# Batch 0's keys and queries loaded in full precision, 4096-byte output rows, and eight SBUF slots for expert weights that are copied or skipped

## The chip, the cores and the metric

The kernel runs on one core of a Trainium2 chip. The metric is device time in microseconds of one execution. The kernel before was run three times: 172.74, 174.44 and 174.59 us, median 174.44 us. One more execution was profiled.

## What is computed

There are two stages. The first is an attention in which 576 positions of each head are first averaged into 32 memory slots:

```python
a = softmax over positions of phi            # (8, 8, 576, 32)
k_m = einsum('bhsm,bhsd->bhmd', a, k)        # 32 averaged keys per head
v_m = einsum('bhsm,bhsd->bhmd', a, v)
attn = softmax(q @ k_m^T / 8)                # 576 x 32 per head
x = (attn @ v_m), heads side by side         # 4608 rows of 512
```

The second is a mixture of experts on the 4608 rows, with a dense branch beside it:

```python
y_dense = relu(x @ w1_dense) @ w2_dense
expert = argmax(x @ w_gate); gate = softmax(x @ w_gate)[expert]
y = y_dense + gate * (relu(x @ w1[expert]) @ w2[expert])
```

There are 8 batches, 8 heads of width 64, and 8 experts with weights 512 x 512. All inputs are float32.

## The kernel before

The work is cut by batch. Every batch goes through the same steps, and each step is a small function that is registered under a name. A long string, ORDER, lists the steps by hand: a token such as hd2:5 is hidden tile 2 of batch 5, and /A or /V picks ScalarE or VectorE for a copy. The program is issued in exactly this order, so the order of tokens is the order within each engine's queue; between engines semaphores decide.

The steps of one batch are these.

- Loads. Lphi (line 164) brings phi over SP's queue in float32. Lq, Lk and Lv (lines 188 and 181) bring q, k, v over the queue of GpSimd (called POOL in the profile), whose DMAs turn float32 into float16 as they go. Each row of such a load has 1152 bytes (phi) or 2304 bytes (q, k, v) at the source.
- e0, e1: ScalarE takes the exponential of phi (line 300). z, kv: TensorE sums it and its products with k and v (lines 311, 333), kvm divides. T, kTc, vTc turn the averaged keys and values (lines 355, 365).
- q0, q1, qT0, qT1: TensorE transposes q, a copy brings it to SBUF (line 114). s0, s1 are the scores (line 412), ET, Z, ln, inv and A their softmax (lines 425, 436, 449, 458, 463). A holds the attention weights; it stands for x, since the weights of the second stage are multiplied with v_m first.
- vg, pc, choose: the logits are vT times the gate weights. choose (lines 501 to 507) sums the logits over all memory slots of the batch and takes the expert with the largest sum. A register is loaded from its result (line 513), and steps w1 and w2 (lines 211, 218) load that expert's two matrices, 512 KB each after the cast, over POOL's queue with a dynamic address. Each matrix has two buffers.
- fd, vd and fe, ve fold v_m with the dense or the expert's first matrix (line 596). hd, Hd and he, He are the hidden layers (lines 609, 650, 652, 663), four tiles of 128 each; He multiplies the gate in. yd and ye are the second matrices (line 683): both halves accumulate into the same PSUM tile p_y of a chunk of 128 rows (the last one has 64). Y copies it to SBUF (lines 707, 709), o stores it over SP's queue (lines 718, 723).
- L, mxeq, ex, gates, pg, gB give the expert of every row, its gate, and whether it is the batch's expert. pn and flags count the rows that chose another one; if there are any, others(b) runs after the main part and adds the other experts' share. On the given inputs it does not run.

The tile pool of PSUM has two double banks ("big": p_q, p_kv, p_s, p_z, p_h, p_g), three single ones ("one": p_vw, p_y) and one small. VectorE, ScalarE and POOL work strictly in the order of their queues: an instruction that waits holds all behind it.

A values_load reads a register of one engine from SBUF. The load of w1 waits for it, and so does every load that stands behind it in POOL's queue.

Of the kernel before, what the change touches and what calls it, by code (L numbers as in the profile page):

```python
# [31 lines left out]
q1:3 He1:1 Lk:3 yd4:1 ye4:1 Lv:3 q0:3 Lphi:3 choose:2 A0:2 ye0:1 A1:2 ye1:1 L:2 Y4:1/A qT1:3/A
Y0:1/A ex:2 Y1:1/V mxeq:2 qT0:3/V hd1:2 yd3:1 yd2:1 e0:3 hd3:2 w1:2 ye3:1 e1:3 z:3 Hd1:2/A Hd3:2/A
gates:2 kv:3 pg:2 ye2:1 rz:3 gB:2/A kvm:3 Y3:1/A T:3 hd0:2 kTc:3/V w2:2 s1:3 Hd0:2/A fe:2 Y2:1/V
vTc:3/V Lq:4 ve1:2/V ET1:3 ve0:2/A hd2:2 s0:3 fd:3 Hd2:2/V vg:3 ET0:3 he2:2 He2:2 Z0:3 vd0:3/A yd0:2
ln0:3 vd1:3/V he0:2 he3:2 He0:2 yd1:2 He3:2 vgc:3 he1:2 Z1:3 pc:3 Lphi:5 Lphi:4 yd4:2 Lphi:6 He1:2
e0:5 ye4:2 inv0:3 e0:4 ye0:2 choose:3 ln1:3 q0:4 q1:4 inv1:3 A0:3 Y4:2/A e1:4 A1:3 Lk:4 qT1:4/V
qT0:4/V yd2:2 Y0:2/A L:3 ex:3 yd3:2 hd2:3 ye3:2 hd0:3 mxeq:3 ye2:2 gates:3 Hd2:3/V pg:3 Hd0:3/V z:4
e1:5 Y3:2/A gB:3/V rz:4 Y2:2/A Lv:4 w1:3 kv:4 kvm:4 hd1:3 hd3:3 T:4 e1:6 Hd1:3/A fe:3 ve1:3/V
kTc:4/V Hd3:3/A ye1:2 ve0:3/A Y1:2/A he3:3 he1:3 vTc:4/V He3:3 vg:4 fd:4 Lk:5 w2:3 He1:3 s1:4 yd4:3  # L40
ET1:4 vgc:4 vd1:4/A s0:4 ET0:4 vd0:4/V Lq:5 pc:4 he0:3 He0:3 yd3:3 Z0:4 ln0:4 inv0:4 he2:3 yd2:3
Lv:5 He2:3 A0:4 choose:4 Z1:4 ye2:3 ye3:3 ln1:4 q1:5 inv1:4 Lq:6 q0:5 A1:4 L:4 Y3:3/A qT1:5/V ex:4
mxeq:4 yd0:3 ye4:3 gates:4 qT0:5/A Y4:3/A kv:5 z:5 pg:4 e0:6 rz:5 yd1:3 kvm:5 gB:4/A T:5 kTc:5/A
Y2:3/V hd0:4 s1:5 ye1:3 ET1:5 vTc:5/V Hd0:4/V Z1:5 vg:5 s0:5 ln1:5 Y1:3/V w1:4 fe:4 hd3:4 ET0:5
# [22 lines left out]
def kernel(  # L67
# [795 lines left out]
```

## Time and profile before

| | |
|---|---|
| runs | 172.74 to 174.59 us, median 174.44 |
| profiled execution | 171.97 us, of which the span from first to last instruction is 170.3 |
| TensorE clock granted | 0.996 |
| TensorE busy | 143.5 us (84%), 2401 matmuls |
| VectorE, ScalarE, POOL busy | 101.0, 88.3, 32.2 us |
| POOL's DMA queue q0 | 22176 packets, 23.60 MB, 83.6% of 16 engines' span |
| SP's DMA queue q1 | 10056 packets, 14.11 MB, 24.0% |
| HBM read and written | 51.92 and 9.44 MB |

Bytes of a queue are counted where they are written, so a casting load counts half of what it reads. DMA shares are sums over packets in flight and can pass 1. PE in the profile is TensorE, PEld its weight load, DVE VectorE, ACT ScalarE.

### The profile page before, as it was taken

How to read it: one execution, taken by the hardware profiler on the slowest of the kernel's cores; microseconds unless marked ns; L12 is line 12 of the kernel's file. 1: busy time of each engine (PE TensorE's matmuls, PEld its weight loads, DVE VectorE, ACT ScalarE, POOL GpSimd, SP SyncE). 2: the span in 40 equal slices, each digit the busy share in tenths (PEclk: the TensorE clock that was granted, in tenths of full speed). 3: DMA queues.
4: the chain of work that ended last, by engine and by line, in shares of the span. 5: the costliest groups of instructions: out<-in, count | busy, mean ns of one | idle time of the engine just before them, and what ended most of it. 6: DMA issues, size and time to landing. Idle time of an engine off the chain costs nothing.

```text
span 170.3 us, 5557 instructions
## 1 busy us (share of the span) xinstructions
PE 143.5 (84%) x2401; PEld 84.8 (50%) x2401; DVE 101.0 (59%) x268; ACT 88.3 (52%) x153; POOL 32.2 (19%) x49
## 2 busy tenths in 40 slices
PE   4013779898999998999999989999699999999960
PEld 3012446465545655556655735565365655456430
DVE  0055275474795863688577856877477756476410
ACT  3130296887236665773666755443574674853130
POOL 7700009002600080008200600080030001200000
PEclk9999999999999999999999999999999999999998
DMA  4999999999999999999999999999999996899461
GB/s 121 300 235 209 206 207 195 205 204 208 199 207 219 246 332 228 243 207 174 203 206 209 187 201 212 289 365 237 208 208 207 259 386 251 111 229 396 190 224 45
DMA packets 32342, 38.18 MB, mean 224 GB/s; under 512 B 1588, under 2 KB 28212, under 8 KB 32312
## 3 DMA queue, kind: packets, MB, share of 16 engines
q0 software_dynamic: 22176, 23.60, 83.6%
q1 hardware_dynamic: 10056, 14.11, 24.0%
q8 instruction: 20, 0.33, 0.7%
q10 hardware_dynamic: 80, 0.07, 0.1%
q14 instruction: 10, 0.08, 0.1%
HBM read 51.92 MB, written 9.44 MB: 360 GB/s over the span
## 4 chain that ended last, share of the span: by engine, by line
PE 54%; DMA 30%; DVE 4%; issue 3%; POOL 2%; ACT 1%; POOLq 1%
PE p_y L683 26%; DMA w1e<-in_moe_w_dram 15%; PE p_h L609 14%; DMA kv<-in_k_dram 8%; DMA w2e<-in_moe_w_dram 7%; PE p_vw L596 3%; PE p_z L436 2%; PE p_s L412 2%; PE p_kv L333 2%; DVE HTe L663 1%; POOL q L188 1%; PE p_g L576 1%; DVE A L463 1%; PE p_q L390 1%; POOLq L513 1%
## 5 line engine op out<-in xcount | busy, mean ns | idle before, releaser
L683 PE MATMUL p_y<-w2d,HTd 128*128 128x512 f16 (+1 forms) x192 | 37.3, 346 | 0.0
L683 PE MATMUL p_y<-w2e,HTe 128*128 128x512 f16 (+1 forms) x192 | 36.7, 345 | 0.6 <-DMA w2e<-in_moe_w_dram 0.6
L663 DVE SCALAR_TENSOR_TENSOR HTe<-p_h,gB 128x576 f16<-128x576 f32 x32 | 23.5, 755 | 12.5 <-PE p_h L609 11.9
L211 POOL DMA_DIRECT2D w1e<-in_moe_w_dram x8 | 6.0, 746 | 112.1 <-DVE A L463 56.0
L609 PE MATMUL p_h<-A,vwd 128*128 128x288 f16 x128 | 22.1, 299 | 0.9 <-DVE qT L114 0.9
L707 ACT ACTIVATE y<-p_y 128x512 f32<-128x512 f32 (+1 forms) x25 | 13.8, 554 | 15.8 <-PE p_y L683 15.2
L683 PEld LDWEIGHTS <-HTe 128*128 128x128 f16 (+1 forms) x192 | 14.6, 101 | 13.7 <-issue 2.5
L683 PEld LDWEIGHTS <-HTd 128*128 128x128 f16 (+1 forms) x192 | 15.1, 101 | 11.6 <-issue 1.3
L609 PE MATMUL p_h<-A,vwe 128*128 128x288 f16 x128 | 19.5, 286 | 0.2 <-DVE HTd L652 0.2
L650 ACT ACTIVATE HTd<-p_h 128x576 f16<-128x576 f32 x21 | 13.4, 649 | 10.2 <-PE p_h L609 8.2
L300 ACT ACTIVATE E<-phi 128x576 f16<-128x576 f32 x16 | 10.5, 679 | 10.2 <-DMA phi<-in_phi_dram 9.5
L609 PEld LDWEIGHTS <-vwe 128*128 128x128 f16 x128 | 11.9, 97 | 5.8 <-issue 1.1
L609 PEld LDWEIGHTS <-vwd 128*128 128x128 f16 x128 | 11.3, 100 | 6.9 <-issue 2.4
L449 ACT ACTIVATE lnz<-p_z 128x576 f32<-128x576 f32 x16 | 10.3, 649 | 8.4 <-PE p_z L436 7.3
L709 DVE TENSOR_SCALAR y<-p_y 128x512 f32<-128x512 f32 (+1 forms) x15 | 9.5, 635 | 7.6 <-PE p_y L683 7.1
L425 ACT ACTIVATE ET<-p_s 128x576 f16<-128x576 f32 x16 | 10.2, 650 | 6.4 <-PE p_s L412 6.4
L114 DVE CAST vwe<-p_vw 128x512 f16<-128x512 f32 x12 | 8.0, 688 | 8.3 <-PE p_vw L596 8.3
L463 DVE TENSOR_TENSOR A<-ET,lnz 128x576 f16<-128x576 f16 x16 | 11.5, 744 | 0.3
L458 ACT ACTIVATE lnz<-lnz 128x576 f32<-128x576 f32 x16 | 10.7, 685 | 0.2
L114 ACT COPY qT<-p_q 128x1152 f16<-128x1152 f16 x7 | 7.7, 1114 | 4.1 <-PE p_q L390 4.1
L333 PE MATMUL p_kv<-kv,E 64*32 64x128 f16 x576 | 6.8, 232 | 3.1 <-DMA kv<-in_k_dram 3.1
L652 DVE TENSOR_SCALAR HTd<-p_h 128x576 f16<-128x576 f32 x11 | 8.3, 755 | 1.9 <-PE p_h L609 1.7
(86 smaller groups left out, 174.6 us busy)
## 6 DMA issues: line engine op xcount, KB each, us to landing
out_dram<-y SPq DMA_DIRECT2D x32, 256.0 KB, 4.8
q<-in_q_dram POOLq DMA_DIRECT2D x8, 576.0 KB, 12.1
kv<-in_v_dram POOLq DMA_DIRECT2D x8, 576.0 KB, 16.2
kv<-in_k_dram POOLq DMA_DIRECT2D x8, 576.0 KB, 14.3
w1e<-in_moe_w_dram POOLq DMA_DIRECT2D x8, 512.0 KB, 7.1
w2e<-in_moe_w_dram POOLq DMA_DIRECT2D x8, 512.0 KB, 11.6
phi<-in_phi_dram SPq DMA_DIRECT2D x7, 576.0 KB, 9.6
out_dram<-y SPq DMA_DIRECT2D x15, 64.0 KB, 4.2
```

What stands on the lines that cost most here:

```text
L114: (nc.scalar.copy if e == "A" else nc.vector.tensor_copy)(out=out, in_=in_)
L300: nc.scalar.activation(out=x["E"][:, :, hs].rearrange("p t j m -> p j t m"), in_=x["phi"][:, hs], func=AF.Exp,)
L333: nc.tensor.matmul(x["kvz"][M * j : M * j + M, a, 0 : 2 * Dh], lhsT=x["E"][rs, t, j], rhs=x["kv"][rs, :, j, t], start=(t == 0), stop=(t == ...
L425: nc.scalar.activation(out=st[b]["ET"][:, a].rearrange("m (p t) -> m p t", t=T), in_=st[b].pop(("ps", a)).rearrange("m (t p) -> m p t", t= ...
L449: nc.scalar.activation(out=st[b]["lnz"][:, a].rearrange("p (h c) -> p h c", h=2), in_=st[b].pop(("pz", a))[:, :, 0:HC], func=AF.Ln,)
L458: nc.scalar.activation(out=lnz, in_=lnz, func=AF.Exp, scale=-1.0)
L463: eng.tensor_mul(out=A[b][:, a], in0=st[b]["ET"][:, a], in1=st[b]["lnz"][:, a])
L609: nc.tensor.matmul(p_h[:, h, 0:HC], lhsT=vw[:, g, 128 * ft : 128 * ft + 128], rhs=a[:, g, HC * h : HC * h + HC], start=(g == 0), stop=(g = ...
L650: nc.scalar.activation(out=o, in_=p_h, func=AF.Relu)
L663: nc.vector.scalar_tensor_tensor(out=x["HTe"][:, ft].rearrange("p (h c) -> p h c", h=2), in0=x.pop(("pe", ft))[:, :, 0:HC], scalar=0.0, in ...
L683: nc.tensor.matmul(p_y[n * u : n * u + n, 0:w], lhsT=HT[:, ft, lo : lo + n], rhs=w2[:, ft, w * u : w * u + w], start=(half == 0 and ft == ...
L707: nc.scalar.activation(out=o, in_=p_y, func=AF.Copy, scale=1.0 / SC)
```

## The change

It has four parts, and the whole ORDER string is new.

1. Batch 0's q and k are no longer loaded by casting DMAs. Steps Fq0, Fq1, Fk0, Fk1 load them in halves in float32 over SP's queue, into buffers of the output tile; Cq0 casts on VectorE, Cq1, Ck0 and Ck1 cast on POOL. For batch 0 the sums over k and v are separate steps (kk, kmk, Tk and vv, kmv, Tv). Seven groups of 8 warm-up matmuls in place of two stand behind z:0. The gate weights are turned by ScalarE.
2. A stored row is 4096 bytes: a partition holds two neighbouring rows of the output. For that, chunk c of 128 rows takes every second of 256 columns of HT and A, and the gates of the chunk are written to PSUM at a stride of two.
3. W1 and W2 hold a slot for each of the 8 batches. choose also looks for the first earlier batch with the same expert; if there is one, both loads of the batch are skipped by a condition on their DMA. Steps rl, cw1 and cw2 then copy, for each batch from 1 on and on VectorE, from the slot found (its own, if nothing was found) to the batch's slot.
4. s0 and s1 become one step, s, with the matmuls of both interleaved. phi has two buffers in place of three, A has two in place of eight, and phi of batches 2, 3, 5, 6, 7 is loaded over POOL's queue. others(b) computes the attention again, as A is not kept.

The start of the new order:

```
Lv:0 Lphi1:0 cblk:0 Fq0:0 Lw1d:0 Lq:1 Lk:1 Lv:1 cid:0 Lwg:0 ciota:0 cones:0 Cq0:0/V Lphi0:0 e1:0
wgt:0/A wgm:0 e0:0 Fk0:0 Ck0:0/P Fk1:0 Ck1:0/P z:0 warm:0/8 warm:0/8 warm:0/8 warm:0/8 warm:0/8
warm:0/8 warm:0/8 rz:0 q0:0 Fq1:0 kk:0 kmk:0 Tk:0 vv:0 qT0:0/A ciotac:0 kTc:0/V wgc:0 kmv:0 Cq1:0/P
q1:0 Tv:0 qT1:0/V vTc:0/A vg:0 s:0 ET1:0 ET0:0 vgc:0 pc:0 Z1:0 fd:0 Z0:0 choose:0 ln1:0 inv1:0 ln0:0
inv0:0 vd0:0/V q0:1 q1:1 A1:0 vd1:0/A A0:0 qT0:1/V qT1:1/V Lphi:1/S hd2:0 e0:1 w1:0 e1:1 Lw2d:0 L:0
hd0:0 Hd2:0/A ex:0 Hd0:0/V mxeq:0 hd3:0 hd1:0 z:1 rz:1 gates:0 Hd3:0/A kv:1 kvm:1 T:1 w2:0 Hd1:0/A
vTc:1/V fd:1 kTc:1/A vd0:1/V s:1 vg:1 vgc:1 Lq:2 ET0:1 ET1:1 fe:0 pc:1 pg:0 vd1:1/A Z0:1 yd1:0
ve1:0/V ve0:0/V gB:0/A ln0:1 he3:0 he0:0 yd0:0 choose:1 He3:0 He0:0 he1:0 Lphi:2/P he2:0 yd3:0 He1:0
He2:0 w1:1 Z1:1 ln1:1 inv1:1 rl:1 inv0:1 A1:1 ye1:0 q0:2 ye3:0 ye0:0 A0:1 Y3:0/A e1:2 L:1 qT0:2/V
Y0:0/V cw1:1 Y1:0/V hd0:1 q1:2 yd4:0 e0:2 ye4:0 qT1:2/A ex:1 Y4:0/A yd2:0 mxeq:1 Hd0:1/A gates:1
...
```

POOL's queue after that holds, in order: w1:1, k:2, v:2, w2:1, phi:3, q:3, k:3, v:3, w1:2, w2:2, q:4, v:4, k:4, phi:5, w1:3, k:5, v:5, q:5, w2:3, w1:4, w2:4, q:6, v:6, phi:6, k:6, q:7, w1:5, w2:5, phi:7, v:7, k:7, w1:6, w2:6, w1:7, w2:7. The copies of w2:3 stand between kv:5 and q1:5 of TensorE's order, and the last tokens are again the store of the short chunk of batch 7.

The core of the diff:

```diff
-    A = [keep.tile([128, 2, S], F16, name=f"A{b}") for b in range(B)]
+    W1 = keep.tile([128, B, DT, F], F16)
+    W2 = keep.tile([128, B, FT, D], F16)
...
+    cols = [slice(256 * (c // 2) + c % 2, 256 * (c // 2) + 256, 2) for c in range(2 * NP)]
+    cols.append(slice(S - 128, S))
...
+    @step("Fk0", "Fk1", "Fq0", "Fq1")
+    def _(b, i, e):
+        if ("f", i[1]) not in st[b]:
+            st[b]["f", i[1]] = wk.tile([128, NJ, T * Dh], F32, tag="y", name="f" + i[1], bufs=NKEEP)
...
+        nc.sync.dma_start(out=st[b]["f", i[1]][:, hs], in_=rows(src[b])[:, hs])
...
+    def load_w1(out, e, cond=None):
         nc.gpsimd.dma_start(
+            out=out, in_=moe_w1[ds(e, 1)].rearrange("o (dt p) f -> p (o dt) f", p=128), cond=cond
...
+        if b and REUSE:
+            same = sm.tile([1, B], F32, tag="same", name="same")
+            nc.vector.scalar_tensor_tensor(
+                out=same[:, 0 : b + 1],
+                in0=em[0:1, 0 : b + 1],
+                scalar=emb[0:1],
+                in1=first[0:1, 0 : b + 1],
+                op0=ALU.is_equal,
+                op1=ALU.mult,
+            )
+            nc.vector.tensor_reduce(out=sel[0:1, 0:1], in_=same[:, 0 : b + 1], axis=AXX, op=ALU.min)
+            nc.vector.tensor_scalar(
+                out=e_i[b][:, 1:2], in0=sel[0:1, 0:1], scalar1=float(B), scalar2=None, op0=ALU.add
+            )
...
+        ev = nc.values_load(e_i[b][:, 0:1], engines=pool, min_val=0, max_val=E - 1)
+        cond = None
+        if b and REUSE:
+            cond = nc.values_load(e_i[b][:, 1:2], engines=pool, min_val=0, max_val=b) >= b
+        st[b]["ev"] = ev, cond
+        load_w1(W1[:, b], ev, cond)
...
+    @step("rl")
+    def _(b, i, e):
+        st[b]["slot"] = nc.values_load(
+            e_i[b][:, 1:2], engines=(ENG.DVE,), min_val=0, max_val=b
+        )
+
+    @step("cw1", "cw2")
+    def _(b, i, e):
+        W = W1 if i == 1 else W2
+        nc.vector.tensor_copy(
+            out=W[:, b].rearrange("p t f -> p (t f)"),
+            in_=W[:, 0 : b + 1][:, ds(st[b]["slot"], 1)].rearrange("p o t f -> p (o t f)"),
+        )
...
+        nc.sync.dma_start(
+            out=out[S * b + 256 * c : S * b + 256 * c + 256].rearrange("(p i) d -> p (i d)", i=2),
+            in_=st[b]["y"][:, 2 * D * c : 2 * D * c + 2 * D],
+        )
```

## The prediction

> **What bounds the kernel now.** I read the page's busy shares first, then fixed stretches of the trace with the busy time of each engine, then the waits of TensorE, then the start instruction by instruction.
>
> ```profile
> PE   4013779898999998999999989999699999999960
> DVE  0055275474795863688577856877477756476410
> DMA  4999999999999999999999999999999996899461
> q0 software_dynamic: 22176, 23.60, 83.6%
> q1 hardware_dynamic: 10056, 14.11, 24.0%
> ```
>
> TensorE and the DMA engines are both full for most of the span. Which of the two sets the pace shows in the stretches (columns: length, then busy time and instructions of PE, weight loads, DVE, ACT, POOL, then clock, DMA share, GB/s as written):
>
> ```profile
> 17.20:25.60 8.40, 6.06 (x184) 3.77 (x185) 4.25 (x12) 4.93 (x9) 0.34 (x1) 1.00 1.22 207
> 25.60:40.00 14.40, 13.10 (x264) 7.90 (x264) 8.54 (x25) 11.17 (x20) 4.11 (x6) 1.00 1.21 202
> 60.00:72.00 12.00, 11.04 (x184) 6.44 (x183) 6.94 (x21) 7.54 (x15) 3.23 (x5) 1.00 1.17 269
> 72.00:100.00 28.00, 28.00 (x536) 16.67 (x535) 21.61 (x59) 17.39 (x32) 7.43 (x10) 1.00 1.20 197
> 100.00:124.00 24.00, 21.62 (x344) 12.71 (x343) 16.12 (x42) 11.56 (x21) 3.71 (x5) 1.00 1.16 257
> 124.00:144.00 20.00, 20.00 (x321) 11.56 (x320) 14.25 (x33) 12.30 (x23) 1.48 (x2) 1.00 1.11 273
> ```
>
> From 72 to 100 and from 124 us to the end TensorE never rests. Its idle time is 17.2 us of start (with some transposes in it), 2.3 us up to 25.6, and after that 1.3 + 0.8 (40 to 60) + 1.0 + 2.4 + 0.1 = 5.5 us. The waits name the cause, and the start shows what its first real work waited for:
>
> ```profile
> PE p_vw L596 <- DMA w1e<-in_moe_w_dram: 3.1, 3, 1.5
> PE p_y L683 <- DMA w2e<-in_moe_w_dram: 0.6, 1, 0.6
> 17.30 1.16 PE L333 MATMUL p_kv<-kv,E 64*32 64x128 f16 x72 [3.12 <-DMA kv<-in_k_dram]
> ```
>
> So the most that could be had is the start, some 5 us of waits for loads, and TensorE's own work.
>
> **What the Trainium skill says.** "DMA: Bandwidth & Descriptors", section Queues, rings and completion order: each DMA engine goes round-robin between queues, packet by packet. The trace agrees:
>
> ```profile
> 3.00:5.00 2.00, 0.07 (x1) 0.00 (x0) 0.00 (x0) 0.00 (x0) 2.00 (x3) 1.00 1.04 369
> 6.00:11.00 5.00, 0.00 (x0) 0.00 (x0) 1.34 (x2) 1.36 (x2) 1.41 (x2) 1.00 1.17 250
> 13.00:17.00 4.00, 1.18 (x73) 1.02 (x65) 2.28 (x10) 0.00 (x0) 0.00 (x0) 1.00 1.22 210
> ```
>
> SP alone moves 369 GB/s (388 in its best us); POOL's casting loads alone write 210, which is 410 to 420 read; together 250, which is a phi row of 1152 B against a key row of 2304 B read and 1152 B written in turn, at some 375 to 380 read. "TensorE: Matmul & The Clock Gate", Part 1: a rested array runs at half clock until some 3.4 us of sustained work. The trace agrees: the same 72 matmuls take 1.16 us at 17.3 and 0.80 at 46.4. "PSUM — Partial Sum Buffer", Specifications: non-contiguous PSUM access slows matmuls; no strided PSUM write is in this trace. "SBUF — State Buffer", Who interferes with whom: a two-port VectorE copy locks GpSimd out for its length; not shown here, and short against the queue's backlog, so nothing.
>
> **The start (early keys, warm-up).** SP now carries phi half, q half, gate weights, phi half, both k halves, the other q half. Its bytes start at about 2.8 us as before; POOL's at about 5 (5.6 by now, its first load issued at 1.53, now 0.6 sooner). Alone at 388 SP brings the first 0.86 MB by 5.1; the phi half (0.29 MB at a third of 380) is there at 7.5; then rows of equal length share evenly, 0.59 MB at 195 GB/s is 3.0 us for each of three halves: 10.5, 13.5, 16.5, plus 0.8 until seen. GpSimd casts each half (1152 per partition): no row here; the "GPSIMD Engine Reference", section 3.1, has 768 ns for 512 elements, so 1.7, with 1.0 (one cycle each) and 2.5 as ends; I take 1.5. Keys are ready at 15.8 (17.2 now), the last q half at 18.8. Then q1 0.7, its copy 0.75, s 0.4, two ET 1.3, ln, inv, ln, inv 2.7, A 0.75: batch 0's A is whole at 25.6, against 26.2 now (25.48 + 0.75). I count **-0.4 us**; the ends of the cast and of POOL's start make it -2 to +2. The 56 warm-up matmuls lie in that wait; the split of k from v adds 72 small ones there, 0.4 us, covered too.
>
> **Order and landings.** At 395 GB/s of reads from 2.8 us I added the loads in both queues' order. On the old order this puts w1 of batch 0 at 31.3 and w2 at 39.4; TensorE took them at 31.7 and 40.0, so the account holds. On the new one: 9.3 MB ahead of w1:0, so 29.7; w2d 32.3; w2:0 34.9 (5 us sooner); w1:1 41.9; v:2 47.7; w2:1 50.3; v:3 60.5; w1:2 63.1; w1:3 about 81; w2:3 91 to 93. Walking the new TensorE order with 0.86 us for a y half, 0.50 for a hidden tile, 0.73 for kv, 0.35 for a fold: kv:2 at 47.9, kv:3 at 62.1 (64.3 now, with one hidden tile less done before it), kv:7 at 128.6 (134.6 now). Visible waits: about 1.0 us for w2d and 2.0 where the copy of w2:3 stands at 90.4. The old order's 5.5 us of waits give way to these 3.0 plus what the copies cost.
>
> **Slots and copies.** The reference on the fixed draw sends the batches to experts 3, 7, 0, 1, 5, 2, 0, 3, so only 6 and 7 skip: 4 loads of 524 KB at 205 GB/s, 10 us of DMA time. They fall after 124 us, where TensorE is idle for 0.1 us: worth **nothing**. The copies run for batches 1 to 7, also from a slot to itself: 14 of 128x2048 f16. "VectorE: DVE Perf Modes", The perf-mode tier table, has 693 ns: 9.7 us; ends 0.69 and 2.29 (no fast mode). Three small operations in choose, about 0.53 a batch (rows of 226, 162, 142 ns). A register load on VectorE, priced from POOL's:
>
> ```profile
> L513 POOLq TENSOR_LOAD <-ei x8: 286/297/858, 23.8 to 142.8; - x8
> L513 POOLq FUSED_REGOPS  x8: 152/152/180, 24.3 to 143.4; - x8
> ```
>
> 0.45 us. Together 2.4 us a batch, 16.6 in all. Off VectorE go 4 Hd (0.755), 3 ve and 2 vd (0.69), 2 kT (0.29) and the gate cast (2.4), onto it 4 y (0.69) and one cast (0.8): -5.9. So 101 becomes 112 us. Behind a waiting copy stand evictions that free p_h and p_y, so TensorE waits after about 1 us. I charge 0.3 us a batch, **1.8**; lower end 0, upper end in the rival. Waits: 3.0 + 1.8 - 5.5 = **-0.7**. POOL has a second register load, 0.45 us, behind a backlog of 5 us or more.
>
> **Matmuls.** s0 and s1 interleaved use both row halves at once: 0.7 us a batch now, perhaps 0.5: **-1.4**, between 0 and -2.4. Gate matmuls write PSUM at a stride (4 of 0.05 us a batch): **+0.4**, 0 to 1.6. Strided weight reads of HT and A: weight loads are 98 ns and busy 50%; nothing.
>
> **Stores.** 16 issues fewer on SP, which waits for y anyway; DMA already reaches 273 GB/s over 124 to 144 and has room at the end (share 0.33 after 164.4): 0, with up to +0.5 since the last full store takes two chunks. phi moved to POOL costs 0.75 us of issue each, five times, in a queue that waits 112 us for choose: 0. Two phi buffers in place of three: phi:2 waits for e0:0 and e1:0, done by 9: 0.
>
> **Sum.** -0.4 - 0.7 - 1.4 + 0.4 = -2.1: span 168.2 for 170.3, the profiled execution 169.9 for 171.97. That one lay 2.5 us under the median of the runs (174.44), so I give 174.44 - 2.1 = **172.3**. This kernel tells about 1% from no change.
>
> **Rivals.** (1) The walk holds with no waits for copies and no new stalls: kv:7 at 128.6 and 31 us of work behind it end TensorE at 159.6 rather than 164.4: 169.5. For: 28 us without a gap at 77% VectorE. Against: the landings leave under 1.5 us at several copies. Chance 0.15. (2) **VectorE becomes the pace-setter**, slower. In 72 to 100 it is busy 21.6 of 28 us; 2.4 us more per 17.5 us, less 0.5 moved away, makes 88%, in strict order, with two copies a batch that hold everything behind them until a load lands. It decides once a copy waits over about 1.5 us or the copies aren't in a fast mode. Half of 1.9 x 7 on TensorE's path is 6.5 for the 1.8 charged: 177; slow copies (14 x 1.6 more, half seen) 188. Against: evictions can slip between. Chance 0.30. (3) What start and order win, the copies' waits take back: 173 to 176, 0.15. (4) The skip doesn't happen: the loads then run as now behind 0.1 us of idle, so the time is that of the forecast; within its share. The forecast, -0.5 to -4, has 0.40.
>
> **Numbers.** Faster by over 1%: 0.15 and 0.30 of the forecast's 0.40: 0.45. Same: the forecast's other 0.10 and 0.10 of (3): 0.20. Slower: 0.30 and 0.05: 0.35. Both signs are likely, so 80% needs 167 to 180; the forecast alone has 170.5 to 174.
>
> **What would show it.** First p_kv at 15.8 with 72 matmuls near 0.8 us; copies at 0.69; DVE near 112 us; q0 at 23.3 MB (23.6, less 2.1 skipped, less 1.2 of early keys and queries, plus 3.0 of phi; 25.4 if nothing is skipped); kv:3 near 62 us; waits of DVE copies for w1 and w2 below 5 us in all. Wrong if copies take over 1.2 us, if TensorE has gaps past 72 us, or if the last q half is seen after 20 us.

## The result and the profile after

The changed kernel took 188.55 us in the median of four runs (183.02 to 192.9); the kernel before took 174.51 us (172.74 to 174.86). It is slower, by a ratio of 1.054 with an interval of 1.041 to 1.068. Two of the four runs were some 9 us longer than the other two, so the ratio is taken from undisturbed runs, which lie at 183 to 184 us; the profiled one took 184.26 us, with a span of 182.6. The forecast was 172.3 us with a range of 167 to 180. The profiled execution before took 171.97, so there are 12.3 us to explain.

The page of the changed kernel has these lines (TensorE's busy time in 40 slices of 4.6 us, then the granted clock, then the DMA engines and POOL's queue):

```profile
PE   0059176979999999999988299996999999999950
PEclk9999955599999999999999669999999999999997
DMA  5999995994999999999999999999907918302861
q0 software_dynamic: 19728, 23.27, 71.0%
```

Two things look new. The clock row falls to half twice, near 23 to 37 and 102 to 108 us. And the DMA row, which was nearly full to the end before, has holes near 27 to 32 and 41 to 46 us and after 133 us; TensorE waits for no load in this execution, so the holes cost it nothing directly. The bytes of q0 are the 23.3 MB forecast (25.37 MB in e8 below, where nothing is skipped), so the skip happens.

The first fall of the clock is not as new as it looks. The clock records of the kernel before begin only at 29.1 us, and its clock row counts the time ahead of the first record as full. Its matmuls say otherwise: the same four matmuls of a hidden tile take 1.04 us at 28.2 and 0.66 at 30.8.

```profile
28.22 1.04 PE L609 MATMUL p_h<-A,vwd 128*128 128x288 f16 x4
30.77 0.66 PE L609 MATMUL p_h<-A,vwd 128*128 128x288 f16 x4
```

So the kernel before also ran at half clock up to some 29 us, and TensorE was busy for 9.5 us of the time from 17.3 on; in the changed kernel it was busy for 10.8 us between 23.2 and 36.8. What is new is the second fall, with 4.3 us of busy time.

The busy time of each engine from the first real work before (17.3 us) to the end of TensorE's work, first before, then after (columns as in the prediction):

```profile
17.30:164.50 147.20, 139.42 (x2288) 81.20 (x2288) 95.61 (x250) 84.61 (x149) 25.98 (x35) 1.00 1.13 230
```

```profile
17.30:176.10 158.80, 144.59 (x2435) 85.13 (x2432) 104.10 (x284) 87.60 (x157) 28.16 (x41) 0.94 0.95 204
```

TensorE ends 11.6 us later. It is busy 5.2 us longer (144.6 less 139.4) and idle 6.4 us longer (14.2 less 7.8); the tail behind it adds 0.7. The half clock accounts for some 2.8 us of the longer busy time. This is an estimate: half of the 15.1 us that TensorE was busy at half clock (10.8 and 4.3), less half of the 9.5 before. The waits of TensorE tell what the idle time is (the first of these lies before 17.3 us):

```profile
PE p_w L293 <- ACT wgt L116: 11.2, 2, 9.1
PE p_kv L357 <- issue: 3.6, 2, 3.3
PE p_q L428 <- issue: 3.6, 2, 3.3
PE p_z L493 <- ACT ET L482: 2.3, 2, 1.7
PE p_h L703 <- DVE qT L116: 1.4, 1, 1.4
```

The waits for expert weights, 3.7 us before, are all gone. In their place stand 7 us marked "issue": time in which TensorE waited for nothing that the profile shows. One of the two long ones, instruction by instruction:

```profile
98.33 0.40 PE L619 MATMUL p_att<-vg,A 128*128 128x8 f16 x10
98.85 0.48 PE L428 MATMUL p_q<-ident,q 64*64 64x64 f16 x36
99.54 0.36 PE L335 MATMUL p_att<-ones,E 128*128 128x2 f16 x9 [0.22 <-ACT ex L642]
99.91 0.80 PE L357 MATMUL p_kv<-kv,E 64*32 64x128 f16 x72
100.64 0.31 PE L428 MATMUL p_q<-ident,q 64*64 64x64 f16 x13
104.20 0.54 PE L428 MATMUL p_q<-ident,q 64*64 64x64 f16 x23 [3.25 <-issue]
```

The gap lies in the middle of a step of 36 equal transposes: 13 run, TensorE stands 3.25 us, 23 run. Before it come 140 small matmuls, each with a weight load, in 2.6 us. And the clock falls to half at 101.7 us, 0.7 us into the gap, and stays there up to 108.5:

```profile
101.00:104.20 3.20, 0.00 (x0) 0.00 (x1) 0.19 (x1) 0.00 (x0) 0.00 (x0) 0.61 1.24 208
104.20:108.50 4.30, 4.30 (x58) 1.87 (x59) 1.71 (x9) 1.60 (x4) 0.00 (x0) 0.50 1.21 211
```

### The profile page after: what moved, and what is told of

The parts are those of the page before. It is cut to its first block, busy times and chain, and to the rows that moved or that the text cites. A ratio compares the mean times of both kernels' runs of the same rounds, so it can differ in the third digit from the quotient of the medians.

```text
span 182.6 us, 5871 instructions
## 1 busy us (share of the span) xinstructions
PE 150.7 (83%) x2513; PEld 91.1 (50%) x2513; DVE 105.9 (58%) x296; ACT 95.1 (52%) x162; POOL 35.7 (20%) x55
## 3 DMA queue, kind: packets, MB, share of 16 engines
q1 hardware_dynamic: 6200, 13.52, 20.9%
## 4 chain that ended last, share of the span: by engine, by line
PE 71%; DMA 8%; ACT 7%; issue 5%; DVE 4%; SPq 1%; ACTq 0%; DVEq 0%
PE p_y L776 33%; PE p_h L703 17%; DMA out_dram<-y 5%; PE p_kv L357 3%; PE p_x L314 3%; PE p_q L428 3%; ACT wgt L116 3%; DMA wgr<-in_moe_w_gate_dram 3%; PE p_vw L690 3%; PE p_z L493 2%; PE p_g L670 2%; PE p_s L470 2%; DVE HTe L757 1%; PE p_att L335 1%; ACT HTd L744 1%
## 5 line engine op out<-in xcount | busy, mean ns | idle before, releaser
L776 PE MATMUL p_y<-W,HTe 128*128 128x512 f16 (+1 forms) x192 | 38.3, 356 | 0.0
L236 POOL DMA_DIRECT2D W<-in_moe_w_dram x8 | 4.6, 574 | 106.6 <-DMA W<-in_moe_w_dram 37.1
L744 ACT ACTIVATE HTd<-p_h 128x576 f16<-128x576 f32 x25 | 15.9, 648 | 13.8 <-PE p_h L703 9.3
L776 PEld LDWEIGHTS <-HTd 128*128 128x128 f16 (+1 forms) x192 | 14.6, 102 | 11.8 <-issue 2.0
L800 ACT ACTIVATE y<-p_y 128x512 f32<-128x512 f32 (+1 forms) x21 | 11.6, 555 | 16.6 <-DMA out_dram<-y 8.2
L802 DVE TENSOR_SCALAR y<-p_y 128x512 f32<-128x512 f32 (+1 forms) x19 | 11.8, 630 | 13.1 <-PE p_y L776 10.2
L703 PEld LDWEIGHTS <-vwd 128*128 128x128 f16 x128 | 12.1, 103 | 7.9 <-issue 3.0
L703 PEld LDWEIGHTS <-vwe 128*128 128x128 f16 x128 | 11.6, 98 | 6.5 <-issue 1.7
L522 DVE TENSOR_TENSOR A<-ET,lnz 128x576 f16<-128x576 f16 x16 | 11.8, 753 | 4.5 <-ACT lnz L515 4.3
L482 ACT ACTIVATE ET<-p_s 128x576 f16<-128x576 f32 x16 | 9.5, 647 | 4.0 <-PE p_s L470 4.0
L428 PE MATMUL p_q<-ident,q 64*64 64x64 f16 x576 | 8.4, 205 | 3.7 <-issue 3.6
L515 ACT ACTIVATE lnz<-lnz 128x576 f32<-128x576 f32 x16 | 10.8, 682 | 0.4
L368 DVE TENSOR_TENSOR kvm<-p_kv,rz 128x256 f16<-128x256 f32 (+1 forms) x9 | 3.5, 394 | 12.7 <-PE p_kv L357 12.6
L357 PE MATMUL p_kv<-kv,E 64*32 64x128 f16 (+1 forms) x648 | 7.7, 225 | 3.7 <-issue 3.6
## 6 DMA issues: line engine op xcount, KB each, us to landing
phi<-in_phi_dram POOLq DMA_DIRECT2D x5, 576.0 KB, 14.2
```

What stands on the lines that cost most here:

```text
L357: nc.tensor.matmul(x["kvz"][M * j : M * j + M, a, Dh * u : Dh * (u + w)], lhsT=x["E"][rs, t, j], rhs=x["kv"][rs, u : u + w, j, t], start=( ...
L428: nc.tensor.transpose(p_q[64 * r : 64 * r + 64, a, P * t : P * t + P], st[b]["q"][rs, 2 * g + (r ^ a), t], ident128[rs, rs],)
L515: nc.scalar.activation(out=lnz, in_=lnz, func=AF.Exp, scale=-1.0)
L522: eng.tensor_mul(out=st[b]["A"][:, a], in0=st[b]["ET"][:, a], in1=st[b]["lnz"][:, a])
L703: nc.tensor.matmul(p_h[:, h, 0:HC], lhsT=vw[:, g, 128 * ft : 128 * ft + 128], rhs=a[:, g, HC * h : HC * h + HC], start=(g == 0), stop=(g = ...
L744: nc.scalar.activation(out=o, in_=p_h, func=AF.Relu)
```

## The experiments

Theory A, at first: TensorE runs out of instructions when many small ones come at once, and then its clock falls. Rival B, from the prediction: VectorE with its copies sets the pace. Each job ran the kernel before on the same chip; its medians were 172.96, 172.94, 172.04, 173.24 and 172.97 us in the five jobs below. It was 174.51 in the first comparison, so times of different jobs are best compared by their ratios to the kernel before; that of the changed kernel is 1.054 [1.041, 1.068].

### First job: gaps, gate cast, warm-up, copies

e1_spread moves one step and two y halves on the changed kernel:

```diff
-... kv:5 cw2:3 q1:5 qT1:5/A ye1:3 kvm:5 T:5 kTc:5/A ye4:3 s:5 vTc:5/A ye0:3 ET1:5
+... kv:5 cw2:3 ye1:3 kvm:5 T:5 kTc:5/A ye4:3 q1:5 qT1:5/A vTc:5/A ye0:3 s:5 ET1:5
```

> The changed kernel with one move in the order: q1 of batch 5 and its copy go behind the two y halves ye1:3 and ye4:3, and ye0:3 goes ahead of s:5, so that the 164 small matmuls from L:4 to q1:5 no longer come in one piece. Nothing is left out. Theory A (TensorE runs out of instructions after some 256 in quick succession, stands 3.3 us, and the rest halves its clock for 6.8 us): the gap at 101 us and the half clock after it go, 4 to 6 us less, so 178 to 180 us where the changed kernel's undisturbed runs have 183.6. Theory B (the copies on VectorE set the pace): nothing of the sort, within 1 us of it. If the gap only moves to another place, A is wrong about what causes it or the move is too small.

e2_wgt_vector turns the gate weights on VectorE again:

```diff
-wgt:0/A wgm:0
+wgt:0 wgm:0
```

> The changed kernel with the two casts of the gate weights back on VectorE, as before the change; nothing is left out. On ScalarE they took 4.7 us ahead of the last exponential of batch 0 (10.8 us). Theory A (the start): that exponential comes at about 8.5, z at 9.5, the 56 warm-up matmuls end by 15 and not 17.4, and the keys' cast on GpSimd (17.1) becomes what kk waits for, so 0.5 to 2.5 us less: 181 to 183 us. Theory B: no effect on the time.

e3_warm2 has two groups of warm-up matmuls for seven:

```diff
-z:0 warm:0/8 warm:0/8 warm:0/8 warm:0/8 warm:0/8 warm:0/8 warm:0/8 rz:0
+z:0 warm:0/8 warm:0/8 rz:0
```

> The changed kernel with 2 groups of 8 warm-up matmuls in place of 7; nothing else is changed. Theory A: the first p_kv no longer waits for warm-up matmuls but for the cast of the keys (17.1), the instruction gap at 19.4 moves behind more real work since 80 instructions are gone, and the clock may start at half: between 2 us less and 1 us more. Theory B: no effect.

e4_no_copy loads every batch's weights and copies none:

```diff
-    REUSE = True
+    REUSE = False
...
 (steps rl, cw1, cw2 left out of the order)
```

> The changed kernel without the reuse: each batch loads its own slot, 16 loads as before, and the 14 copies, the 7 register loads on VectorE and the three small operations in choose are left out; the rest of the order, the early keys and the stores are kept. Theory B (VectorE is the pace-setter): 15 us less work for VectorE give 5 us or more, 178 us or less. Theory A: the copies hid beside a full TensorE and the four loads skipped were worth nothing, so within 1.5 us of 183.6.

| | median (range), us | ratio to before | longest issue gaps, us |
|---|---|---|---|
| e1_spread | 181.55 (181.0 to 182.06) | 1.052 [1.045, 1.060] | 3.04 at 23, 1.76 at 104 |
| e2_wgt_vector | 182.62 (182.02 to 185.0) | 1.058 [1.048, 1.068] | 3.01 at 21, 3.27 at 104 |
| e3_warm2 | 185.0 (183.74 to 187.88) | 1.069 [1.057, 1.081] | 4.01 at 23, 2.16 at 106, 2.44 at 124 |
| e4_no_copy | 190.31 (188.27 to 194.76) | none given | 3.20 at 22, 3.17 at 106 |

A is half borne out: in e1, parting the bunch shortened the gap from 3.25 to 1.76 us and left no half clock after it. But its time missed the 178 to 180 us that A had given, and its ratio, like that of e2, is the changed kernel's within the intervals. And the gaps wander when instructions are added or taken away (e3). That pointed to a count.

e4 was missed by both theories: B had said 178 us or less, and A within 1.5 us of 183.6. It does not clear the copies by itself, since it changes two things, taking the copies away and letting all loads run; e8 below prices the second. What speaks against B as the pace-setter is the trace of the changed kernel: from 17.3 us on, TensorE waits 3.2 us for VectorE in all, where it waited 1.8 before, and the copies themselves wait 0.1 us. No run takes the copies alone away.

### Second job: a bunch in the old kernel, fewer instructions at the start, no skip

e5_before_bunch puts the four steps of batch 5 together in the kernel before:

```diff
-... ln1:4 q1:5 inv1:4 Lq:6 q0:5 A1:4 L:4 Y3:3/A qT1:5/V ex:4
-mxeq:4 yd0:3 ye4:3 gates:4 qT0:5/A Y4:3/A kv:5 z:5 pg:4 e0:6 rz:5
+... ln1:4 inv1:4 Lq:6 A1:4 Y3:3/A yd0:3 ye4:3 L:4 q0:5
+mxeq:4 ex:4 z:5 qT0:5/A rz:5 kv:5 q1:5 qT1:5/V gates:4 Y4:3/A pg:4 e0:6
```

> The kernel before, with only five positions of its order changed: in batch 4/5 the two y halves stand ahead of L:4, and q0:5, z:5, kv:5, q1:5 follow each other, so that about 300 instructions of TensorE (weight loads counted) come in under 3 us, as they do near 100 us in the changed kernel. Theory A (TensorE runs out of instructions after some 250 in quick succession, stands some 3 us, and its clock then halves for one or two periods of 3.4 us): a gap of 2 to 3.5 us marked issue near 95 to 100 us, records at half clock after it, and 2 to 6 us more than the kernel before (175 to 179). Rival (VectorE, slots and copies set the pace; the bunch alone does nothing): no such gap, 172 to 174.

e6_joint_kv joins batch 0's sums:

```diff
-kk:0 kmk:0 Tk:0 vv:0 qT0:0/A ciotac:0 kTc:0/V wgc:0 kmv:0 Cq1:0/P q1:0 Tv:0 qT1:0/V
+kv:0 kvm:0 T:0 qT0:0/A ciotac:0 kTc:0/V wgc:0 Cq1:0/P q1:0 qT1:0/V
```

> The changed kernel with batch 0's sums over k and v joined again in one step (72 matmuls of 128 columns for 2 x 72 of 64), as they stood before; some 150 instructions of TensorE fewer at the start. Theory A: the gap of 3.3 us marked issue at 22.7 us goes or shrinks to under 1.5, the keys' kv:1 (35.5 us) comes 2 to 4 us sooner, and the time falls by 2 to 4 us (about 180 to 182), with the second gap at 104 us left. Rival (the start waits for loads and casts): kv:1 is within 1 us of 35.5 and the time within 1 us of the changed kernel's (about 183.5 undisturbed).

e7_joint_spread_wgt is e1, e2 and e6 together.

> Three edits together on the changed kernel: k and v summed jointly for batch 0, q1:5 parted from kv:5 by two y halves, gate weights turned on VectorE. Theory A: both issue gaps under 2 us, no half clock after 90 us, TensorE busy 145 to 147 us for 150.7, time 176 to 179. If nothing but these gaps and the clock made the kernel slower, it comes to 174 to 176; what is left above the kernel before is then owed to waits for buffers, copies and loads. Rival B (copies on VectorE): 182 or more.

e8_no_skip makes the condition always true:

```diff
-... engines=pool, min_val=0, max_val=b) >= b
+... engines=pool, min_val=0, max_val=b) >= 0
```

> The changed kernel with the condition of the expert loads made always true: all 16 loads run, and the 14 copies stay (for batches 6 and 7 from the slot found, over the batch's own load). The order without copies and skips took 190.3 us, about 5 more than the changed kernel. If the four loads at the end are on the path (batches 6 and 7 wait for weights there), this one takes 187 to 191 and TensorE waits 2 us or more for W after 145 us. If the skip is worth nothing, as predicted, it stays at 183 to 185, and the order without copies lost its 5 us elsewhere (clock and instruction gaps).

e5 took 175.02 us (174.36 to 176.32), ratio 1.021 [1.012, 1.031]. It has no issue gap at the bunch; where it loses time, by its profile, is a wait of TensorE of 2.19 us for gm, after which the clock was at half for 3.4 us. So a bunch alone isn't enough. (By the count that is found below, the limit between two blocks of 256 lies at 97.8 us here, inside the bunch, so that neither block was used up quickly.) e6 took 180.89 us (177.62 to 182.53), ratio 1.056 [1.045, 1.067]: in its profile the gap at 22 us shrank from 3.31 to 1.31, the one at 103 to 0.41, though nothing near 103 had been touched, and one of 2.29 us appeared at 119. e7 took 180.69 (179.77 to 181.93), ratio 1.054 [1.045, 1.064], and has 2.53 us at the same place, 119.6. Theory A had said 176 to 179 for it: a miss. By the ratios, neither gained anything that is clear of noise.

e8 took 197.09 us (193.44 to 201.55): the copies in place, all loads run, and 10 us more than the changed kernel's 183 to 184 even in its shortest run. Two lines from its waits (a long execution, 201.55 us):

```profile
DVE W L608 <- DMA W<-in_moe_w_dram: 7.2, 3, 4.3
PE p_vw L690 <- DVE W L608: 3.1, 1, 3.1
```

In the changed kernel the copies waited 0.1 us in all. With the loads not skipped, copies wait 7.2 us for landings and hold VectorE, and TensorE stands 3.1 us for a copy and 2.3 for a transposed key behind one. So the skip is worth about 10 us to this order: it puts the copies of batch 6 right behind its w1 and w2, where a load that lands some 8 us later can't be waited for. e4, with loads and without copies, shows the same from the other side: TensorE waits 2.32 us for W at 152.8. It is also some 7 us shorter than e8 (190.31 for 197.09, in two jobs). So where all loads run, copies that wait do seem to cost time, as B has it; in the changed kernel they hardly wait.

### What the gaps have in common

I then counted TensorE's instructions (matmuls, weight loads and the few others that the trace lists) against the packets of queue q8, which carries instructions: 16 KB each, one for every 256 instructions. TensorE always stopped 63 instructions short of a multiple of 256: at 449 and 3265 in the changed kernel, 449 and 3777 in e6. The times, from the trace's records:

| kernel | block of 256 used from | its next packet | TensorE goes on | in all |
|---|---|---|---|---|
| changed | 17.47 | 20.38 to 21.26 | 22.73 | 5.26 |
| changed | 98.86 | 101.86 to 102.80 | 104.20 | 5.34 |
| e6 | 16.73 | 19.82 to 20.70 | 22.21 | 5.48 |
| e6 | 114.27 | 116.84 to 117.80 | 119.05 | 4.78 |

The next packet starts 2.6 to 3.1 us after TensorE begins on a block, and TensorE goes on 1.3 to 1.5 us after it has landed. The same holds in every trace of this case. The twenty of them have 37 gaps of TensorE marked issue, from 0.23 to 4.01 us. Every one stands 63 instructions short of a multiple of 256, and every one ends 1.1 to 1.6 us after such a packet has landed. Theory C: a block of 256 instructions that is used up in less than about 5 to 6 us ends in a gap. The Trainium skill, "Runtime: NRT & Kernel Launch", section Instruction fetch mechanics, has the block of 256 instructions and the prefetch of one block ahead, and calls its cost "mostly hidden". The trace agrees on the block; hidden it isn't when a block is used up in 2 us, as at 17.47 and 98.86.

### Third job: the count put to the test

e9_before_64 and e10_before_8 add tiny matmuls to the kernel before, while TensorE is idle:

```diff
-warm:0/8 warm:0/8 e1:1 wgt:0
+warm:0/8 warm:0/8 tiny:0/64 e1:1 wgt:0
...
+    @step("tiny")
+    def _(b, i, e):
+        p_x = one.tile([128, 512], F32, tag="one", name="p_t")
+        for _ in range(int(e)):
+            nc.tensor.matmul(p_x[0:32, 0:2], lhsT=onesb[:, 0:32], rhs=onesb[:, 0:2], start=True, stop=True)
```

> The kernel before with 64 tiny matmuls (32 weights, 2 columns each; 128 instructions with their weight loads) added at its start, while TensorE waits for the gate weights; nothing else differs. Theory C: TensorE's instructions come in blocks of 256, the next block is asked for when the last one begins to be used and is there about 5.9 us later, so TensorE stands whenever a block is used up sooner. 128 instructions more move the limits of all blocks. Counting the blocks over the order of this kernel gives no stand above 0.6 us after 40 us as it was, and with the shift two: 2.3 us near 103 and 2.5 us near 121 us, each marked issue and followed by a period at half clock. Time 177 to 180 for 173. Rival (the stands belong to the changed order or to loads in flight, not to a count of instructions): no gap, 172 to 174.

> The same with 8 tiny matmuls (16 instructions): the control. Theory C: by the same count no stand above 0.5 us after 40 us, the one of 0.8 us near 51 us falls to 0.2 to 0.4, time as the kernel before or up to 0.6 us less (172 to 173.5). Rival: the same time.

e11_parted is the changed kernel with e2's and e6's edits, contiguous chunks (as in e12), and the small steps parted by the count of blocks:

```diff
+tiny:0/20
...
-inv0:4 w1:4 e1:5 A1:4 ... He2:3 q0:5 mxeq:4 He0:3 ex:4 z:5 qT0:5/A rz:5 kv:5 cw2:3 q1:5 qT1:5/A
+inv0:4 q0:5 qT0:5/A q1:5 qT1:5/A w1:4 e1:5 A1:4 ... He2:3 mxeq:4 He0:3 ex:4 z:5 rz:5 kv:5 cw2:3
...
-... Y2:3/V Lq:7 ... yd0:4 q1:6 He3:4 qT1:6/V ... kv:6 o0:3 q0:6 ye4:4 rz:6 kvm:6 qT0:6/V T:6 ... ye3:4
+... Y2:3/V q1:6 qT1:6/V Lq:7 ... yd0:4 He3:4 ... kv:6 o0:3 ye4:4 rz:6 kvm:6 ye3:4 q0:6 qT0:6/V T:6
```

> The changed kernel with batch 0's k and v summed jointly, gate weights turned on VectorE, contiguous chunks with rows of 2048 bytes stored, and q0:5, q1:5, q1:6, q0:6 moved apart from kv:5 and kv:6, plus 20 tiny matmuls at the start, so that by the count of theory C no block of 256 is used up in under 5.5 us after 40 us. Theory C: no gap marked issue above 0.6 us after 40 us and no half clock there, TensorE busy about 145 us, time 173 to 176: level with the kernel before, within 2%. Rival (copies on VectorE, waits for loads): 180 or more, with gaps released by other engines.

e12_rows2048 undoes part 2 alone:

```diff
-    cols = [slice(256 * (c // 2) + c % 2, 256 * (c // 2) + 256, 2) for c in range(2 * NP)]
+    cols = [slice(128 * c, 128 * c + 128) for c in range(2 * NP)]
...
-            out=out[...].rearrange("(p i) d -> p (i d)", i=2),
+            out=out[...].rearrange("(i p) d -> p i d", i=2),
```

> The changed kernel with only part 2 undone: a chunk is 128 neighbouring rows, gates are written to PSUM without a stride, a store writes rows of 2048 bytes (same number of stores). Writing the gates took 6.7 us of TensorE in the changed kernel and 4.6 before. If the stride is the cause, it falls back to 4.6 and the time by 1 to 2.5 us from 183.5, unless the gaps move; if rows of 4096 bytes are worth something in the stores, waits for y buffers grow and part of that is given back.

| | median (range), us | ratio to before |
|---|---|---|
| e9_before_64 | 173.95 (173.41 to 177.68) | 1.010 [1.003, 1.018] |
| e10_before_8 | 173.88 (172.96 to 174.34) | 1.011 [1.005, 1.017] |
| e11_parted | 181.65 (179.16 to 182.79) | 1.057 [1.048, 1.066] |
| e12_rows2048 | 188.41 (187.62 to 190.19) | 1.097 [1.086, 1.108] |

The two gaps of e9 are there, in a kernel whose work and order are the old one's; e10 has none, and the old one at 51 us is gone from it too. TensorE's timeline in e9:

```profile
100.33 0.20 PE L582 MATMUL p_g<-ident,gm 128*128 128x64 f16 x1 [0.74 <-issue]
115.28 0.70 PE L339 MATMUL p_kv<-kv,E 64*32 64x128 f16 x60
116.58 0.29 PE L339 MATMUL p_kv<-kv,E 64*32 64x128 f16 x12 [0.60 <-issue]
```

The second splits a step of 72 equal matmuls into 60 and 12. Place and number are as counted (103 and 121 us were expected), but the size is 0.7 and 0.6 us for 2.3 and 2.5, no half clock follows, and the time is that of the control, not the 177 to 180 us expected: blocks took 4.67 and 3.94 us here. So the count settles where the gaps lie; how long a fetch takes differs between kernels and was not settled.

e11 shows the cure. Its trace has no issue gap at all, and the clock row of its page no half clock after 40 us:

```profile
PEclk9999955869999999999999999999999999999998
```

TensorE's busy time after 17.3 us is 139.4 us, that of the kernel before. But the time is 181.65, where 173 to 176 had been expected: TensorE is now idle 13.9 us, and the waits are these.

```profile
PE p_z L499 <- ACT ET L488: 3.0, 3, 1.7
PE p_q L434 <- POOL q L207: 2.9, 1, 2.9
PE p_att L394 <- DVE kvm L374: 1.7, 2, 1.2
PE p_h L709 <- DVE qT L116: 1.4, 1, 1.4
PE p_h L709 <- ACT qT L116: 1.3, 2, 0.9
```

The pair that prices the gaps is e12 and e11, of one job. Both store rows of 2048 bytes, and e11 differs by the small steps parted, the edits of e2 and e6, and 20 tiny matmuls. Their ratios are 1.097 and 1.057, with intervals well apart: some 4%, of which the start has a share. Against the changed kernel itself e11 gained nothing, since it also gave up part 2. The gaps and the clock are thus part of the loss, and not all of it.

e12 was a surprise: the gate matmuls cost 1.8 us less of TensorE (4.9 for 6.7), yet it is slower than the changed kernel by some 4 us (its shortest runs, 187.6, against 183.0). The gaps were as before; TensorE waited 3.88 us at 130.7 behind ScalarE, whose y eviction waited 4.64 us for a store; in the changed kernel these two were 1.73 and 2.50 us.

### Fourth and fifth jobs: the start, the stores, and parts alone

e13_parted_4096 is e11 without e12's edit:

> e11_parted with rows of 4096 bytes again (strided chunks, as in the changed kernel): everything else as there. If the rows of 4096 bytes are worth what undoing them cost alone (4 to 5 us in e12_rows2048, of which 2 to 3 in clock and gaps), the wait of ScalarE before ET near 123 us (1.73) falls below 1 and the time by 1 to 4 us from 181.65, to 177 to 180, though writing the gates costs 1.9 us more. If it is 181 or more, the store rows are worth nothing once the gaps are gone.

e14_parted_early0 moves three stores on top of that:

```diff
-o4:3
+o1:0 o0:0 o4:0 o4:3
...
 (taken from their old places near the end)
```

> e13_parted_4096 with the three stores of batch 0 moved from the end of the order to the place just ahead of the first store of batch 3, so that a y buffer is free before batch 4 needs one. If waits for y buffers hold ScalarE near 120 us, those (2 to 5 us of waits of y evictions for stores) go and the time falls by 1 to 2.5 us; if the stores only collide there with the loads, it is the same or up to 2 us more.

e16_old_start undoes part 1 alone; e15_parted_old_start does so on e13:

```diff
-Lv:0 Lphi1:0 cblk:0 Fq0:0 Lw1d:0 ... Cq0:0/V Lphi0:0 e1:0 wgt:0/A wgm:0 e0:0 Fk0:0 Ck0:0/P Fk1:0 Ck1:0/P
-z:0 (7 x warm:0/8) rz:0 q0:0 Fq1:0 kk:0 kmk:0 Tk:0 vv:0 ...
+Lphi1:0 cblk:0 Lq:0 Lv:0 Lk:0 Lw1d:0 ... warm:0/8 warm:0/8 Lphi0:0 e1:0 wgt:0 wgm:0 e0:0
+q0:0 qT0:0/A q1:0 qT1:0/V z:0 rz:0 kv:0 kvm:0 T:0 ciotac:0 kTc:0/V wgc:0 ...
```

> The changed kernel with part 1 alone undone: q and k of batch 0 over casting DMAs at the head of POOL's queue, 16 warm-up matmuls, gate weights on VectorE, k and v summed jointly. The old start had the first p_kv at 17.3 and kv:1 at 29.2 us. If the new start is what keeps kv:1 at 33 to 35 us in all variants, kv:1 comes at 30 to 31 here and the time is 177 to 180, with the gap near 100 us still in. If it is the order behind the start, kv:1 stays at 33 or later and the time at 181 or more.

> e13_parted_4096 with the old start as in e16_old_start, and 60 tiny matmuls in place of 20, so that the blocks of instructions lie as in e13. If gaps, clock and start are all of it, 172 to 175, level with the kernel before within 1.5%; if a rest stays that belongs to the new order (waits for y, copies), 176 or more.

e17_before_s and e18_before_4096 put parts 4 and 2, each alone, into the kernel before:

```diff
-s1:5 ... s0:5        (of every batch, at the place of the first)
+s:5
```

```diff
+    cols = [slice(256 * (c // 2) + c % 2, 256 * (c // 2) + 256, 2) for c in range(NCH - 1)]
...
-            nc.sync.dma_start(out=dst, in_=y[:, 0:D])
+                nc.sync.dma_start(
+                    out=out[r : r + 256].rearrange("(p i) d -> p (i d)", i=2),
+                    in_=st[b]["y"][:, 2 * D * (c // 2) : 2 * D * (c // 2) + 2 * D],
```

> The kernel before with s0 and s1 of each batch joined in one step s (part 4 alone), at the place of the first of the two. If the interleaved score matmuls take 4.4 us of TensorE for 7.6, as in the changed kernel, TensorE is busy about 3 us less, and as it sets the pace from 72 us on, the time falls by 1 to 3 us (170 to 172 for 173). If s has to wait for both big PSUM banks at once, that is lost again: 172.5 to 174.

> The kernel before with rows of 4096 bytes stored (part 2 alone): chunk c takes every second of 256 columns, one store of 512 KB for two chunks, at the place of the later one. Writing the gates takes 2 us more of TensorE, which sets the pace: 0.5 to 2.5 us more (173.5 to 175.5), unless the rows help the loads beside them; undoing the same part in the changed kernel cost 4 to 5 us, so a gain there would have to come from shorter waits for y buffers, which this kernel doesn't show: none expected.

| | median (range), us | ratio to before |
|---|---|---|
| e13_parted_4096 | 180.49 (178.56 to 181.49) | none given |
| e14_parted_early0 | 183.45 (182.68 to 185.05) | 1.067 [1.053, 1.081] |
| e16_old_start | 179.43 (175.41 to 186.06) | 1.025 [1.006, 1.044] |
| e15_parted_old_start | 178.46 (177.49 to 181.26) | 1.036 [1.024, 1.047] |
| e17_before_s | 175.55 (173.09 to 179.99) | 1.015 [1.011, 1.019] |
| e18_before_4096 | 180.45 (179.03 to 182.73) | 1.040 [1.033, 1.047] |

The old start brings kv:1, at 35.5 us in the changed kernel and 32 to 36 in every variant of its start, to 30.8 in e16 and e15, and e16's ratio is 1.025 for 1.054. But the four times of e16 lie between 175.4 and 186.1 us (the trace is of the longest), its interval overlaps that of the changed kernel, and where the small steps are parted the old start brought 2 us, inside the spread (e15 against e13). So the sign of this gain is likely, and its size is open. e15, with start and gaps both mended, is not better than e16 within the intervals, and still 6 us behind: a rest belongs to the new order itself. e13 is 1 us better than e11, inside the spread, so the larger rows that were worth 4 us against e12 are worth nothing clear once the gaps are gone; e14's early stores met the loads (a wait for k of 1.11 us at 85, one of 1.68 behind a copy at 90) and cost 3 us, the opposite of what was hoped.

e17 and e18 bear on two steps of the sum. Joined scores took 5.7 us of TensorE for 7.6, but the kernel became slower, where a gain of 1 to 3 us or none had been expected. And e18's larger stores, good for 4 us in the changed order, cost 4% in the old one:

```profile
65.09 0.80 PE L340 MATMUL p_kv<-kv,E 64*32 64x128 f16 x72 [2.11 <-DMA kv<-in_v_dram]
126.84 0.63 PE L603 MATMUL p_vw<-w1e,vT 64*32 64x512 f16 x8 [4.75 <-DMA w1e<-in_moe_w_dram]
```

In the kernel before, the wait for w1e at this place was 1.51 us and the one for v under 0.3. This suggests that stores at other moments, of other length, delay the loads beside them. It is not parted from the other effect of this edit, gates that take 2.9 us more of TensorE. (This execution took 182.73 us.)

## Why the prediction was wrong

**The start, -0.4 us: failed.** The casts on GpSimd took 1.14 to 1.15 us (1.5 taken), but the arrivals were late: keys ready at 17.1 (15.8), the last q half at 20.2 (18.8; after 20 was one of the prediction's own signs of being wrong). And batch 0's A was whole at 30.3 us, not 25.6 (the steps listed there add up to 25.4); it was 26.2 before, so 4.1 us were lost where 0.4 had been counted as won. The sentence that failed is "the 56 warm-up matmuls lie in that wait; the split of k from v adds 72 small ones there, 0.4 us, covered too". What lay there was not covered:

```profile
17.36 0.48 PE L428 MATMUL p_q<-ident,q 64*64 64x64 f16 x36
17.76 0.75 PE L357 MATMUL p_kv<-kv,E 64*32 64x64 f16 x72
19.12 0.30 PE L357 MATMUL p_kv<-kv,E 64*32 64x64 f16 x30
22.73 0.49 PE L357 MATMUL p_kv<-kv,E 64*32 64x64 f16 x42 [3.31 <-issue]
```

The gate cast, counted only as a relief of VectorE, took 4.7 us on ScalarE ahead of e0, and with it z and the warm-up matmuls, which ended at 17.4, 0.3 us after the keys were there. The 72 extra matmuls are 144 extra instructions: q, kk and the first of vv use a block up in 2.0 us, and TensorE stands 3.3 us. The half clock from 23.2 on is no third loss, since the kernel before was at half clock there too.

The runs part the two. Without an issue gap at the start, A is whole at 28.1 us (e7, e11, e13); there TensorE waits 1.5 to 2.9 us for the last q half instead, which is ready at 20.9 to 21.2. With the old start A is whole at 25.6 (e15, e16). So of the 4.7 us by which A missed the forecast, the gap, together with the gate cast that these three also undo, cost some 2.2 and the late q half the rest. Undone alone, the gate cast brought A forward to 29.0 us and left the ratio where it was (e2, 1.058).

**Order, landings and waits, -0.7 us: the waits were right in sign, the sum failed.** It counted 3.0 us of waits for loads in place of 5.5; TensorE waited for none. The term that was put at nothing, without a reason, is the supply of instructions: 7 us of issue gaps, and a second fall of the clock behind one of them (gaps past 72 us were the other sign of being wrong that came). kv:7 came at 143.3 us for 128.6; 4.7 us of this were there at A already.

**The clock.** The prediction held it at full speed once warm, and did not see that the kernel before, with TensorE busy for 9.5 of 11.8 us from 17.3 on, stayed at half clock up to 29.1. "TensorE: Matmul & The Clock Gate", section HAM oscillation, gives the rule of no idle gap over some 3.4 us. These traces differ from it. After 40 us, eleven of twelve gaps of 2.4 to 4.75 us had a record at half clock of 3.4 or 6.8 us that began in the gap or within 1.5 us of its end (for the twelfth, in e8, it began 1.9 us after); of sixteen between 1.5 and 2.35 us five had one. In e14 and e15 the clock fell behind two gaps of only 0.9 and 0.8 us, which e11 and e13 have without a fall. So the length of one gap does not decide it. Every change of the clock in the twenty traces lies a whole number of 3.41 us after the first one of its trace. That would fit a decision by how busy TensorE was over a fixed stretch of time; no run tests it.

**Slots: copies right, skip wrong.** The line of the copies:

```profile
L608 DVE COPY W<-W 128x2048 f16 x14 | 9.5, 687 | 0.1
```

687 ns for the 693 taken, VectorE at 105.9 us (112 forecast), and 0.1 us of waiting. "Worth nothing" for the skip was argued from the old order, where TensorE had no idle time after 124 us. The new order leans on it: e8 lost 10 us.

**Scores, -1.4 us (0 to -2.4): the size was off, and it was no gain in time.** They took 4.4 us of TensorE for 7.6, so -3.2. Alone in the old kernel they made it slower by 1.5% (e17). What took it back was not settled. In that profile (an execution of 177.34 us) the wait for qT at 26.4 is 1.60 us, for 0.86 at this place before, and there is one of 0.61 for ET at 145 that the kernel before has not; s needs both halves of q and both banks at once, which would fit.

**Gates, +0.4 us (0 to 1.6): mis-sized.** 6.7 us for 4.6 is +2.1, and 7.5 in e18; undoing the stride brought it back to 4.9.

**Stores, 0 to +0.5: failed in both directions.** They are worth 4 us in the new order (e12), nothing clear in the parted one (e13 against e11), and cost 4% in the old one (e18), the gates included each time.

**The rivals.** None named the cause. Rival 2 had the right side; its mechanism, copies that wait and hold VectorE, is not in the changed kernel (0.1 us of waiting) and shows only where all loads run (e8). Rival 1 had the waits for loads and copies right and TensorE's end 16 us too early. Rival 4 held the skip to change nothing; without it e8 is 10 us longer.

**What stays open.** About 6 us remain with start and gaps mended (e15): 2 us of gates, two periods of 3.4 us at half clock, and waits behind ScalarE and VectorE, which differ from order to order. How these add up was not tested. No version tried beats the kernel before.

## What to carry to other kernels

Count instructions as well as their time: a stretch of small matmuls that uses up 256 TensorE instructions, weight loads included, in under 4 to 6 us can end in a gap whose place is set by a count from the start of the program, so that an edit at 10 us moves a stall at 100 us. An "issue" gap inside a run of equal matmuls is its sign, and parting small steps by large ones removed it here (e11). Price a part in the order that it will run in: the larger stores gained in one order and lost in another, and the skip, priced at nothing from the old order, is worth some 10 us in the new one.

## What the runs showed of the hardware that was not expected

- All 37 issue gaps of TensorE in the twenty traces stand 63 instructions before a multiple of 256 and end 1.1 to 1.6 us after the landing of a 16 KB packet. From the first instruction of such a block to the first of the next it took 3.9 to 6.8 us in all but one (9.6, in e17).
- 128 added tiny matmul instructions at the start made two gaps of 0.74 and 0.60 us some 95 and 110 us later.
- The clock fell to half behind eleven of twelve gaps of TensorE from 2.4 us on, behind one of 1.55 us, and behind two of 0.9 and 0.8 us; it changed only at whole multiples of 3.41 us after its first record.
- Where a trace's first clock record comes late (29.1 us before), the time ahead of it is shown at full clock though TensorE ran at half.
- The cast of 4x512 f32 to f16 with a turned access pattern took 2.37 us on ScalarE for 1.42 us on VectorE.
- GpSimd cast 128x1152 from f32 to f16 in 1.15 us.
